# Product of ab with the combined weights: blocks of 480, 192 and 480 tokens in place of four of 288

## Chip, cores and metric

One core of one Trainium2 chip. The time is device microseconds (us) of one execution, median over runs; before the change it is 621.64 us (three runs, 618.79 to 622.22). Lower is better.

## What is computed

Attention over 2 batches, 8 heads and 576 tokens (local for half of the heads, strided for the others) gives x with 1152 rows, the tokens of both batches one after the other, and 512 columns. Two mixtures follow:

```python
a = x @ w1                      # 1152 x 1024
b = x @ w2
x = ((a * b) @ w3) @ w_out      # 1152 x 512
p = probs / (probs.sum(-1, keepdims=True) + 1e-9)
out = 0
for e in range(4):
    out += p[:, e:e+1] * (relu(x @ e1[e]) @ e2[e])
```

## The kernel before

Everything runs on one core in an order written out by hand (a manual schedule): each engine executes its instructions in the order in which the program issues them. Every float32 product is made of three matmuls (`mm3`, lines 303 to 305) on a high and a low part (`hi`, `lo`, type float32r): hi by hi, hi by lo, lo by hi, each with a weight load of its own of 128 x 128. ScalarE (ACT) rounds a number to its high part (a CAST), VectorE (DVE) subtracts it from the number, which leaves the low part.

The stages, with their place in the span:

- Attention, until about 85 us, mixed with the first half of the next stage.
- ab = a * b, feature-major, in units of one block of 128 features (`ft`, 8 of them; two make a *pair*) and half a batch of tokens (288): `ab_block`. A unit is 24 matmuls of 288 columns in two accumulators (`ab_acc`). ACT copies the first one out (L566), DVE multiplies the second one by it (L568), ACT and DVE split the product (L572, L574) into the tile of its batch and pair, `ab_parts`. For pairs 0 to 2 of batch 0 the product is kept whole at first and split later, while batch 1 is computed (`ab_split`, L531 and L532, 1152 columns at once, after units 18, 21 and 24 of 32). Between these operations the program issues, by `advance`, steps of the decoding of the weights that come next: for each 1024-column chunk two ACT operations (L142, L147), DVE's clamp, shift, sign and add (L183, L186, L189, L193), and the split (L201, L230). The raw chunk comes by DMA into one of two buffers, and its load is issued when the add of an earlier chunk is done.
- wc = the product of w3 and w_out (`wc_tile`, 8 tiles of 24 matmuls of 512 columns), 142 to 186 us.
- x3 = wc by ab (`x3_block`), 186 to 237 us: 4 blocks of 288 tokens by 4 blocks of output features, each 8 `ft` by 3 matmuls of 288 columns into one accumulator (`x3_acc`, shown as x_acc in the profile), copied out by ACT (L596). In the last two blocks of tokens the operands of the next stage's first half (tokens 0 to 639) are prepared between them (`early`, 11 steps of splits and subtractions, L616, L617, L621).
- The experts (`Step.first` and `Step.second`), 237 to 613 us, in two halves of 640 and 512 tokens: matmuls of 320 or 256 columns and of 512 columns, with the decoding of the expert weights beside them.

Accumulators of ab, wc and x3 come from one pool of 5 PSUM banks, in turn (`bank`): the sixth accumulator waits until the first of the six has been read. The tiles `ab_parts` lie in two pools of 4 (`big[0]` on the right for batch 0, `big[1]` on the left for batch 1); `big[0]` is released for the operands of the experts (`ops`) when its part of x3 is done.

Of the kernel before, what the change touches and what calls it, by code (L numbers as in the profile page):

```python
# [8 lines left out]
F32 = mybir.dt.float32  # L9
F32R = mybir.dt.float32r  # L10
# [4 lines left out]
ALU = mybir.AluOpType  # L15

B, H, S, D = 2, 8, 576, 64
NT, DM, DFF, E = 1152, 512, 1024, 4
P = 128
# [5 lines left out]
T3 = 3 * NB  # L25
CUT = 288
HB = S // 2
BLK = 384
NBLK = NT // BLK
NTT = NT // P  # L30
# [12 lines left out]
def kernel(  # L43
# [13 lines left out]
    nc = tc.nc  # L57
# [10 lines left out]
    big = [tc.tile_pool(name=f"big{b}", bufs=4, side=side).__enter__() for b, side in enumerate(("right", "left"))]  # L68
# [3 lines left out]
    def bank(name):  # L72
        return ps.tile([P, 512], F32, tag="ps", name=name)

    def unit(name, dtype=F32R):
        return wp.tile([P, 1024], dtype, tag="w", name=name)
# [51 lines left out]
    class Chunk:  # L128
# [68 lines left out]
        def split_hi(self):  # L197
            nonlocal live
            live += 2
            self.hi, self.lo = unit("w_hi"), unit("w_lo")  # L200
            nc.scalar.copy(self.hi, self.f32)  # L201
# [27 lines left out]
        def split_lo(self):  # L229
            nc.vector.tensor_tensor(out=self.lo, in0=self.f32, in1=self.hi.bitcast(F32), op=ALU.subtract)  # L230
            self.done = True
# [61 lines left out]
    def advance(n=1):  # L293

        return all([next(worker, False) for _ in range(n)])
# [5 lines left out]
    def mm3(acc, lhs, rhs, first, last):  # L301
        (lh, ll), (rh, rl) = lhs, rhs
        mm(acc, lh, rh, start=first, stop=False)  # L303
        mm(acc, lh, rl, start=False, stop=False)  # L304
        mm(acc, ll, rh, start=False, stop=last)  # L305
# [212 lines left out]
                nc.vector.tensor_tensor(out=lo, in0=o, in1=hi.bitcast(F32), op=ALU.subtract)  # L518


    ab_hi, ab_lo, whole = {}, {}, {}

    def ab_place(b, pair):
        both = big[b].tile([P, 2, 2, S], F32R, tag="big", name="ab_parts")
        ab_hi[b, pair], ab_lo[b, pair] = both[:, 0], both[:, 1]

    def ab_split(pair):

        ab_place(0, pair)
        hi, lo, ab = ab_hi[0, pair], ab_lo[0, pair], whole.pop(pair)  # L530
        nc.scalar.copy(hi, ab)  # L531
        nc.vector.tensor_tensor(out=lo, in0=ab, in1=hi.bitcast(F32), op=ALU.subtract)  # L532

    def x_split_hi(n):
        x = slice(n * HB, n * HB + HB)
        nc.scalar.copy(x_hi[:, :, x], x_whole[:, :, x])

    def x_split_lo(n):
        x = slice(n * HB, n * HB + HB)
        nc.vector.tensor_tensor(out=x_lo[:, :, x], in0=x_whole[:, :, x], in1=x_hi[:, :, x].bitcast(F32),  # L540
                                op=ALU.subtract)

    def ab_block(b, ft, n):
        t = slice(b * S + n * HB, b * S + n * HB + HB)
        pair, late = ft // 2, b == 0 and ft < 6
        ab = tmp.tile([P, HB], F32, tag="pT", name="ab")
        if n == 0 and ft % 2 == 0:
            if late:
                if pair < 2:
                    parts = big[pair].tile([P, 2, 2, S], F32, tag="big", name="ab_f32")  # L550
                    whole[pair] = parts[:, 0]
                    if pair:
                        whole[2] = parts[:, 1]
            else:
                ab_place(b, pair)
        if late:
            full = whole[pair][:, ft % 2, n * HB:n * HB + HB]
        else:
            full = ab
            hi, lo = (x[b, pair][:, ft % 2, n * HB:n * HB + HB] for x in (ab_hi, ab_lo))  # L560
        for w in range(2):
            acc = bank("ab_acc")[:, :HB]
            for k in range(4):
                mm3(acc, c_w12[ft].parts((w * 4 + k) * P, P), (x_hi[:, k, t], x_lo[:, k, t]), k == 0, k == 3)
            if w == 0:
                nc.scalar.copy(ab, acc)  # L566
            else:
                nc.vector.tensor_tensor(out=full, in0=acc, in1=ab, op=ALU.mult)  # L568
            yield
        if late:  # L570
            return
        nc.scalar.copy(hi, ab)  # L572
        yield
        nc.vector.tensor_tensor(out=lo, in0=ab, in1=hi.bitcast(F32), op=ALU.subtract)  # L574
        yield


# [9 lines left out]
        nc.scalar.copy(raw[:, it], acc)  # L587


    def x3_block(x3, wc, b, n, ot):  # L590
        t = slice(b * S + n * HB, b * S + n * HB + HB)
        acc = bank("x3_acc")[:, :HB]
        for k in range(8):
            ab = tuple(x[b, k // 2][:, k % 2, n * HB:n * HB + HB] for x in (ab_hi, ab_lo))
            mm3(acc, wc[k // 2].parts(512 * (k % 2) + ot * P, P), ab, k == 0, k == 7)
        nc.scalar.copy(x3[:, ot, t], acc)  # L596


# [217 lines left out]
    with tc.manual_schedule():  # L816
# [24 lines left out]
        def run_unit():  # L841

            nonlocal done, rest
            b, ft, i = units[done]
            if done >= 2:
                need(c_w12[ft])
            block = ab_block(b, ft, i)
            for _ in range(2):
                next(rest, None)
                next(block)  # L850
                if done >= 2:
                    advance(1)
                if waiting:
                    waiting.pop().slots_exps()
            rest = block
            done += 1
            if b == i == 1:
                c_w12[ft].free()
# [129 lines left out]
        for n in range(2):  # L988
            acc = bank("ab_acc")[:, :HB]
# [23 lines left out]
        while done < 32:  # L1013
            run_unit()
            if done in (18, 21, 24):
                ab_split({18: 0, 21: 1, 24: 2}[done])
# [7 lines left out]
        wc = [Chunk(None) for _ in range(4)]  # L1024
        for c in c_wout:
            need(c)
        for it in range(8):
# [8 lines left out]
            i = {1: 0, 3: 1, 6: 2}.get(it)  # L1036
# [7 lines left out]
        x3 = xp.tile([P, 4, NT], F32, tag="x_lo", name="x3")  # L1044
# [8 lines left out]
                return kept[:, k]  # L1053
            return ops.tile([P, 2, 320], F32R, tag="op", name=f"b_{name}{i}")[:, :, :n]

        for b, i in ((0, 0), (0, 1), (1, 0), (1, 1)):
            if (b, i) == (1, 0):
                big[0].release()
                ops = ctx.enter_context(tc.tile_pool(name="ops", bufs=14, side="right"))
                early = halves[0].prepare(x3)  # L1060
            for ot in range(4):
                x3_block(x3, wc, b, i, ot)
                advance(1)
                if (b, i) == (1, 0) and ot < 2:
                    next(early)
                elif (b, i) == (1, 1):
                    for _ in range(4):
                        next(early, None)
        for c in wc[:3]:
# [18 lines left out]
        for s, step in enumerate(steps):  # L1088
            need(step.w, 1)
            before = steps[s - 1] if s else None  # L1090
            todo = iter(range(len(before.half.tts)) if s else ())
# [86 lines left out]
```

## Time and profile before

| | us |
|---|---|
| time, median of 3 runs | 621.64 (618.79 to 622.22) |
| the profiled execution, its own time | 618.11 |
| its span, first to last instruction | 616.3 |
| TensorE (PE) busy in the span | 610.0 |
| weight loads (PEld) busy, beside PE | 555.9 |
| VectorE (DVE) busy | 442.4 |
| ScalarE (ACT) busy | 279.3 |

The difference of 1.8 us between the execution's time and its span lies around the span. Matmuls are pipelined, so that the duration of one (0.29 us at 288 columns) is longer than the distance from its start to the next one's (0.13 us): a stage's time is read from starts. Weight loads overlap with matmuls in the same way.

### The profile page before, as it was taken

The page shows a single profiled execution, that of the slowest core. Times are in us where ns is not written, and L with a number is a line of the kernel's source. Part 1 is how long each engine was busy: PE and PEld are TensorE (multiplying, and loading weights), DVE is VectorE, ACT ScalarE, POOL GpSimd, SP SyncE. Part 2 cuts the span into 40 slices and gives each one's busy share as a digit, 9 for nine tenths or more (in the row PEclk, how much of TensorE's full clock was granted, in tenths as well). Part 3 has the DMA queues.
Part 4 walks back from the last instruction along what each step waited for, and adds up shares of the span by engine and source line. Part 5 has one row for each costly group of instructions (what it writes and reads, how often), then busy time and mean ns, then how long its engine had stood idle before and what let it go on. Part 6 is the DMA issues. An engine that isn't in the chain of part 4 may idle for free.

```text
span 616.3 us, 11292 instructions
## 1 busy us (share of the span) xinstructions
PE 610.0 (99%) x4584; PEld 555.9 (90%) x4584; DVE 442.4 (72%) x796; ACT 279.3 (45%) x555; POOL 9.1 (1%) x33
## 2 busy tenths in 40 slices
PE   9999999999999999999999999999999999999997
PEld 5789999998889999998899998999889898989997
DVE  4899987898774237777877987887766665755843
ACT  4779966665644224333443433434343333333320
POOL 4100000000000000000000000000000000000000
PEclk9999999999999999999999999999999999999999
DMA  8986340334524102333545344445585657465411
GB/s 262 350 290 188 139 138 2 112 129 150 198 98 137 58 12 69 137 136 138 194 155 192 124 157 171 160 148 200 188 311 211 213 194 244 166 231 180 151 54 69
DMA packets 28403, 99.44 MB, mean 161 GB/s; under 512 B 2632, under 2 KB 6288, under 8 KB 25920
## 3 DMA queue, kind: packets, MB, share of 16 engines
q1 hardware_dynamic: 28080, 98.43, 45.4%
q8 instruction: 36, 0.59, 0.4%
q10 hardware_dynamic: 272, 0.29, 0.1%
q14 instruction: 15, 0.12, 0.1%
HBM read 79.58 MB, written 19.14 MB: 160 GB/s over the span
## 4 chain that ended last, share of the span: by engine, by line
PE 89%; DVE 4%; ACT 2%; DMA 2%; issue 1%; SPq 0%; POOL 0%; POOLq 0%; ACTq 0%
PE g_acc L303 11%; PE g_acc L304 11%; PE g_acc L305 11%; PE m_a L305 4%; PE m_a L304 4%; PE m_a L303 4%; PE ab_acc L303 4%; PE ab_acc L305 4%; PE ab_acc L304 4%; PE m_b L304 3%; PE m_c L303 3%; PE x_acc L305 3%; PE x_acc L303 3%; PE x_acc L304 3%; PE m_c L304 3%; PE m_b L303 3%
## 5 line engine op out<-in xcount | busy, mean ns | idle before, releaser
L725 ACT ACTIVATE h_hi<-u 128x320 fp32r<-128x320 f32 (+1 forms) x128 | 57.0, 446 | 189.1 <-DVE u L731 189.1
L303 PE MATMUL g_acc<-w_hi,h_hi 128*128 128x512 f32 (+1 forms) x296 | 114.3, 386 | 0.0
L304 PE MATMUL g_acc<-w_lo,h_hi 128*128 128x512 f32 (+1 forms) x296 | 114.2, 386 | 0.0
L305 PE MATMUL g_acc<-w_hi,h_lo 128*128 128x512 f32 (+1 forms) x296 | 113.7, 384 | 0.0
L664 DVE TENSOR_TENSOR w_lo<-raw,w_hi 128x768 fp32r<-128x768 f32 x64 | 69.4, 1085 | 12.5 <-ACT w_hi L662 12.4
L731 DVE TENSOR_TENSOR u<-m_b,u 128x320 f32<-128x320 f32 (+1 forms) x96 | 40.8, 453 | 50.8 <-PE m_b L305 50.8
L303 PE MATMUL ab_acc<-x_hi,w_hi 128*128 128x288 f32 x240 | 71.7, 299 | 0.1
L305 PE MATMUL ab_acc<-x_hi,w_lo 128*128 128x288 f32 x240 | 70.8, 295 | 0.7 <-DVE w_lo L230 0.7
L304 PE MATMUL ab_acc<-x_lo,w_hi 128*128 128x288 f32 x240 | 70.7, 294 | 0.0
L305 PEld LDWEIGHTS g_acc<-w_hi,h_lo 128*128 128x128 f32 x296 | 55.6, 188 | 11.6
L303 PEld LDWEIGHTS g_acc<-w_hi,h_hi 128*128 128x128 f32 x296 | 55.8, 188 | 8.0
L304 PEld LDWEIGHTS g_acc<-w_lo,h_hi 128*128 128x128 f32 x296 | 55.7, 188 | 7.6
L727 DVE SCALAR_TENSOR_TENSOR h_lo<-u,h_hi 128x320 fp32r<-128x320 f32 (+1 forms) x128 | 57.8, 451 | 3.7 <-ACT h_hi L725 1.8
L662 ACT CAST w_hi<-raw 128x768 fp32r<-128x768 f32 x64 | 60.0, 938 | 0.0
L305 PEld LDWEIGHTS ab_acc<-x_hi,w_lo 128*128 128x128 f32 x240 | 45.0, 188 | 1.0 <-DVE w_lo L230 1.0
L303 PEld LDWEIGHTS ab_acc<-x_hi,w_hi 128*128 128x128 f32 x240 | 45.0, 188 | 0.6 <-ACT pT L461 0.4
L304 PEld LDWEIGHTS ab_acc<-x_lo,w_hi 128*128 128x128 f32 x240 | 45.0, 188 | 0.0
L304 PE MATMUL m_b<-b_t,s_hi 128*128 128x320 f32 (+1 forms) x128 | 37.9, 296 | 0.0
L731 DVE TENSOR_TENSOR u<-m_a,u 128x320 f32<-128x320 f32 (+1 forms) x64 | 28.9, 452 | 11.6 <-PE m_a L305 11.6
L664 DVE TENSOR_TENSOR s_lo<-raw,s_hi 128x1024 fp32r<-128x1024 f32 x16 | 19.6, 1226 | 24.4 <-ACT s_hi L662 24.4
L731 DVE TENSOR_TENSOR u<-m_c,u 128x320 f32<-128x320 f32 (+1 forms) x64 | 29.0, 454 | 4.5 <-PE m_c L305 3.9
L741 ACT COPY u<-m_a 128x320 f32<-128x320 f32 (+1 forms) x32 | 12.8, 400 | 41.9 <-PE m_a L305 41.9
(178 smaller groups left out, 1412.8 us busy)
## 6 DMA issues: line engine op xcount, KB each, us to landing
raw<-in_e_dram SPq DMA_DIRECT2D x32, 1024.0 KB, 5.3
raw<-in_w3T_dram SPq DMA_DIRECT2D x8, 1024.0 KB, 5.6
stored<-s_hi SPq DMA_DIRECT2D x16, 512.0 KB, 2.7
stored<-s_lo SPq DMA_DIRECT2D x16, 512.0 KB, 2.7
s_hi<-stored SPq DMA_DIRECT2D x16, 512.0 KB, 5.0
s_lo<-stored SPq DMA_DIRECT2D x16, 512.0 KB, 5.6
raw<-in_w_dram SPq DMA_DIRECT2D x7, 1024.0 KB, 7.2
raw<-in_w_out_dram SPq DMA_DIRECT2D x4, 1024.0 KB, 5.0
```

The lines of the kernel that those rows point to most:

```text
L303: mm(acc, lh, rh, start=first, stop=False)
L304: mm(acc, lh, rl, start=False, stop=False)
L305: mm(acc, ll, rh, start=False, stop=last)
L662: nc.scalar.copy(dst[0], src)
L664: nc.vector.tensor_tensor(out=dst[1], in0=src, in1=dst[0].bitcast(F32), op=ALU.subtract)
L725: nc.scalar.activation(hi, src, AF.Relu)
L727: nc.vector.scalar_tensor_tensor(out=lo, in0=src, scalar=0.0, in1=hi.bitcast(F32), op0=ALU.max, op1=ALU.subtract)
L731: nc.vector.tensor_tensor(out=out, in0=acc, in1=b, op=ALU.add)
L741: nc.scalar.copy(u1, a)
```

## The change

The 1152 tokens of x3 are taken in three blocks: 0 to 479, 480 to 671 and 672 to 1151. The middle block crosses the border of the batches at 576. So that its 192 tokens are side by side in SBUF for one matmul, pairs 0 to 2 keep the last 96 tokens of batch 0 and the first 96 of batch 1 in a tile of their own (`middle`), which is the rest of a batch's `ab_parts` tile once its other 480 tokens are placed: the tile of batch 0 holds the middle of the pair's second `ft`, that of batch 1 that of its first. Pair 3 is stored as before, and takes two matmuls of 96 columns in the middle block. A split of a unit whose tokens lie on both sides of the new border is done in two pieces (96 and 192 columns), the late splits in three (96, 96 and 960).

```diff
+MID = 192
+MAIN = S - MID // 2
...
     def ab_place(b, pair):
-        both = big[b].tile([P, 2, 2, S], F32R, tag="big", name="ab_parts")
-        ab_hi[b, pair], ab_lo[b, pair] = both[:, 0], both[:, 1]
+        both = big[b].tile([P, 4 * S], F32R, tag="big", name="ab_parts")
+        n = MAIN if pair < 3 else S
+        parts_of[b, pair] = both[:, :4 * n].rearrange("p (x k n) -> p x k n", x=2, k=2)
+        if pair < 3:
+            middle[pair, 1 - b] = both[:, 4 * n:].rearrange("p (x n) -> p x n", x=2)
+
+    def ab_pieces(b, ft, t0, n):
...
+    def split_hi(pieces, src):
+        for at, x in pieces:
+            nc.scalar.copy(x[:, 0], src[:, at])
+
+    def split_lo(pieces, src):
+        for at, x in pieces:
+            nc.vector.tensor_tensor(out=x[:, 1], in0=src[:, at], in1=x[:, 0].bitcast(F32), op=ALU.subtract)
...
     def ab_split(pair):
         ab_place(0, pair)
-        hi, lo, ab = ab_hi[0, pair], ab_lo[0, pair], whole.pop(pair)
-        nc.scalar.copy(hi, ab)
-        nc.vector.tensor_tensor(out=lo, in0=ab, in1=hi.bitcast(F32), op=ALU.subtract)
+        if (1, pair) not in parts_of:
+            ab_place(1, pair)
+        ab, main = whole.pop(pair), parts_of[0, pair]
+        for k in range(2):
+            nc.scalar.copy(middle[pair, k][:, 0, :MID // 2], ab[:, k, MAIN:])
+        nc.scalar.copy(main[:, 0], ab[:, :, :MAIN])
+        for k in range(2):
+            x = middle[pair, k][:, :, :MID // 2]
+            nc.vector.tensor_tensor(out=x[:, 1], in0=ab[:, k, MAIN:], in1=x[:, 0].bitcast(F32), op=ALU.subtract)
+        nc.vector.tensor_tensor(out=main[:, 1], in0=ab[:, :, :MAIN], in1=main[:, 0].bitcast(F32), op=ALU.subtract)
...
-    def x3_block(x3, wc, b, n, ot):
-        t = slice(b * S + n * HB, b * S + n * HB + HB)
-        acc = bank("x3_acc")[:, :HB]
-        for k in range(8):
-            ab = tuple(x[b, k // 2][:, k % 2, n * HB:n * HB + HB] for x in (ab_hi, ab_lo))
-            mm3(acc, wc[k // 2].parts(512 * (k % 2) + ot * P, P), ab, k == 0, k == 7)
+    def x3_block(x3, wc, i, ot):
+        t0, n = ((0, MAIN), (MAIN, MID), (MAIN + MID, MAIN))[i]
+        t = slice(t0, t0 + n)
+        acc = bank("x3_acc")[:, :n]
+        todo = []
+        for ft in range(8):
+            w = wc[ft // 2].parts(512 * (ft % 2) + ot * P, P)
+            pair, k = ft // 2, ft % 2
+            if pair == 3:
+                for b in range(B):
+                    a, z = max(t0, b * S), min(t0 + n, b * S + S)
+                    if a < z:
+                        todo.append((w, slice(a - t0, z - t0), parts_of[b, pair][:, :, k, a - b * S:z - b * S]))
+            else:
+                todo.append((w, slice(0, n), middle[pair, k] if i == 1 else parts_of[i // 2, pair][:, :, k]))
+        for i, (w, at, x) in enumerate(todo):
+            mm3(acc[:, at], w, (x[:, 0], x[:, 1]), i == 0, i == len(todo) - 1)
         nc.scalar.copy(x3[:, ot, t], acc)
...
-        for b, i in ((0, 0), (0, 1), (1, 0), (1, 1)):
-            if (b, i) == (1, 0):
+        for i in range(3):
+            if i == 2:
                 big[0].release()
...
             for ot in range(4):
-                x3_block(x3, wc, b, i, ot)
-                advance(1)
-                if (b, i) == (1, 0) and ot < 2:
-                    next(early)
-                elif (b, i) == (1, 1):
+                x3_block(x3, wc, i, ot)
+                advance(1 if i == 1 else 1 + ot % 2)
+                if i == 2:
                     for _ in range(4):
                         next(early, None)
```

On PE, in the x3 stage, before the change, the end of one accumulator's 24 matmuls and the start of the next one's (names with their numbers; `wc_hi` is the last quarter of the combined weights):

```order
L303 MATMUL x3_acc_2499<-ab_parts_1411,wc_hi_2451 128x288
L304 MATMUL x3_acc_2499<-ab_parts_1411,wc_hi_2451 128x288
L305 MATMUL x3_acc_2499<-ab_parts_1411,wc_lo_2452 128x288
L303 MATMUL x3_acc_2526<-ab_parts_1668,w_hi_2279 128x288
L304 MATMUL x3_acc_2526<-ab_parts_1668,w_hi_2279 128x288
L305 MATMUL x3_acc_2526<-ab_parts_1668,w_lo_2280 128x288
```

On PE after the change, where the first block of 480 ends and the middle block begins, then where its pairs 0 to 2 end and pair 3 begins:

```order
L305 MATMUL x3_acc_2613<-ab_parts_1411,wc_hi_2475 128x480
L306 MATMUL x3_acc_2613<-ab_parts_1411,wc_hi_2475 128x480
L307 MATMUL x3_acc_2613<-ab_parts_1411,wc_lo_2476 128x480
L305 MATMUL x3_acc_2642<-ab_parts_1607,w_hi_2303 128x192
L306 MATMUL x3_acc_2642<-ab_parts_1607,w_hi_2303 128x192
...
L307 MATMUL x3_acc_2642<-ab_parts_1916,w_lo_2480 128x192
L305 MATMUL x3_acc_2642<-ab_parts_1411,wc_hi_2475 128x96
L306 MATMUL x3_acc_2642<-ab_parts_1411,wc_hi_2475 128x96
L307 MATMUL x3_acc_2642<-ab_parts_1411,wc_lo_2476 128x96
L305 MATMUL x3_acc_2642<-ab_parts_2080,wc_hi_2475 128x96
L306 MATMUL x3_acc_2642<-ab_parts_2080,wc_hi_2475 128x96
L307 MATMUL x3_acc_2642<-ab_parts_2080,wc_lo_2476 128x96
```

Each row is one weight load and one matmul. The stage had 16 accumulators of 24 matmuls, 384 of 288 columns. It has 8 accumulators of 24 matmuls of 480 columns and 4 of 18 matmuls of 192 and 12 of 96, together 312: 192 of 480, 72 of 192 and 48 of 96. The columns streamed are the same, 110,592.

On ACT in batch 1's part of the ab stage, around the late split of pair 2, before:

```order
L531 CAST ab_parts_1900<-ab_f32_833 128x1152
L572 CAST ab_parts_1748<-ab_1863 128x288
L566 COPY ab_1904<-ab_acc_1906 128x288
L201 CAST w_hi_1920<-t_1820 128x1024
L572 CAST ab_parts_1905<-ab_1904 128x288
```

and after (L551 stands for L572, L564 and L565 for L531, L603 for L566, L203 for L201):

```order
L564 CAST ab_parts_1917<-ab_f32_833 128x96
L564 CAST ab_parts_1916<-ab_f32_833 128x96
L565 CAST ab_parts_1916<-ab_f32_833 128x960
L551 CAST ab_parts_1756<-ab_1878 128x288
L603 COPY ab_1925<-ab_acc_1926 128x288
L203 CAST w_hi_1940<-t_1834 128x1024
L551 CAST ab_parts_1917<-ab_1925 128x96
L551 CAST ab_parts_1917<-ab_1925 128x192
```

The same happens at the late splits of pairs 0 and 1 and at the first half of every `ft` of pairs 0 to 2 of batch 1: 3 by 2 and 6 by 1, 12 operations more on ACT, and the 12 subtractions that belong to them on DVE. SP's and POOL's instructions stay in their order.

## Rows read from the trace of the kernel before

**Rows 1.** The page: busy shares, then the chain that ended last by engine.

```profile
span 616.3 us, 11292 instructions
PE 610.0 (99%) x4584; PEld 555.9 (90%) x4584; DVE 442.4 (72%) x796; ACT 279.3 (45%) x555; POOL 9.1 (1%) x33
...
PE 89%; DVE 4%; ACT 2%; DMA 2%; issue 1%; SPq 0%; POOL 0%; POOLq 0%; ACTq 0%
```

**Rows 2.** The x3 stage as one window: us, busy of each engine, granted clock, DMA.

```profile
185.74:236.63 50.89, 50.89 (x386) 50.88 (x384) 18.41 (x25) 16.03 (x29) 0.00 (x0) 1.00 0.17 63
```

**Rows 3.** Timeline of PE: start, us; matmuls of 512, 288, 320 and 256 columns.

```profile
179.62 0.39 PE L303 MATMUL wc_acc<-w_hi 128*128 128x512 f32 x1
...
185.75 0.29 PE L303 MATMUL x_acc<-ab_parts,w_hi 128*128 128x288 f32 x1
...
236.63 0.31 PE L303 MATMUL m_a<-b_b,w_hi 128*128 128x320 f32 x1
...
240.88 0.31 PE L305 MATMUL m_b<-b_t,s_lo 128*128 128x320 f32 x1
...
575.90 0.28 PE L303 MATMUL m_a<-kept,w_hi 128*128 128x256 f32 x1
...
578.74 0.40 PE L303 MATMUL g_acc<-w_hi,h_hi 128*128 128x512 f32 x1
```

**Rows 4.** Timeline of the weight loads, at two places where matmuls had paused.

```profile
33.68 0.19 PEld L303 LDWEIGHTS ab_acc<-x_hi,w_hi 128*128 128x128 f32 x1
33.79 0.19 PEld L304 LDWEIGHTS ab_acc<-x_lo,w_hi 128*128 128x128 f32 x1
...
142.05 0.19 PEld L303 LDWEIGHTS wc_acc<-w_hi 128*128 128x128 f32 x1
142.16 0.19 PEld L304 LDWEIGHTS wc_acc<-w_lo,w_hi 128*128 128x128 f32 x1
```

**Rows 5.** Timeline of PE: 16 plain float32 products of 288 columns, two records each.

```profile
22.61 8.03 PE L581 MATMUL ab_acc<-x_whole,w_whole 128*128 128x288 f32 x32
```

**Rows 6.** A window of the ab stage, columns as in rows 2.

```profile
105.00:115.00 10.00, 10.00 (x77) 10.00 (x77) 9.94 (x15) 7.65 (x12) 0.00 (x0) 1.00 0.01 2
```

**Rows 7.** Timeline of DVE and of ACT, a split and what follows it.

```profile
111.83 0.45 DVE L574 TENSOR_TENSOR ab_parts<-ab,ab_parts 128x288 fp32r<-128x288 f32 x1
112.20 0.45 DVE L568 TENSOR_TENSOR ab<-ab_acc,ab 128x288 f32<-128x288 f32 x1
...
112.68 0.43 ACT L572 CAST ab_parts<-ab 128x288 fp32r<-128x288 f32 x1 [1.26 <-DVE ab L568]
113.02 0.39 ACT L566 COPY ab<-ab_acc 128x288 f32<-128x288 f32 x1
```

**Rows 8.** All splits of 1152 columns, by line.

```profile
L531 ACT CAST ab_parts<-ab_f x3: 1152/1159/1162, 96.5 to 120.8; 128x1152 fp32r<-128x1152 f32 x3
L532 DVE TENSOR_TENSOR ab_parts<-ab_f,ab_parts x3: 1351/1359/1359, 98.4 to 121.9; 128x1152 fp32r<-128x1152 f32 x3
```

**Rows 9.** Timeline of ACT, DVE and PE at the end of the ab stage.

```profile
134.36 1.19 ACT L142 ACTIVATE raw<-raw 128x1024 int32<-128x1024 uint32 x1 [2.75 <-DMA raw<-in_w3T_dram]
...
136.80 0.38 ACT L566 COPY ab<-ab_acc 128x288 f32<-128x288 f32 x1
...
141.54 0.45 DVE L568 TENSOR_TENSOR ab<-ab_acc,ab 128x288 f32<-128x288 f32 x1
...
137.26 0.37 PE L303 MATMUL ab_acc<-x_hi,w_hi 128*128 128x288 f32 x1
137.47 0.29 PE L304 MATMUL ab_acc<-x_lo,w_hi 128*128 128x288 f32 x1
...
142.11 0.44 PE L303 MATMUL wc_acc<-w_hi 128*128 128x512 f32 x1
```

**Rows 10.** Timeline of ACT and DVE at the end of the x3 stage.

```profile
234.55 0.73 ACT L616 CAST b_t<-x 128x640 fp32r<-128x640 f32 x1 [0.52 <-DVE x L621]
...
235.31 0.82 DVE L617 TENSOR_TENSOR b_t<-x,b_t 128x640 fp32r<-128x640 f32 x1 [0.79 <-ACT b_t L616]
```

More of the change, by code (lines that the diff above doesn't have):

```diff
@@ L518, in put_lo @@
                 nc.vector.tensor_tensor(out=lo, in0=o, in1=hi.bitcast(F32), op=ALU.subtract)
-    ab_hi, ab_lo, whole = {}, {}, {}
+    parts_of, middle, whole = {}, {}, {}
     def ab_place(b, pair):
-        both = big[b].tile([P, 2, 2, S], F32R, tag="big", name="ab_parts")
-        ab_hi[b, pair], ab_lo[b, pair] = both[:, 0], both[:, 1]
+        both = big[b].tile([P, 4 * S], F32R, tag="big", name="ab_parts")
[3 more added lines that the diff above has]
+            middle[pair, 1 - b] = both[:, 4 * n:].rearrange("p (x n) -> p x n", x=2)
@@ new lines, in ab_pieces @@
+    def ab_pieces(b, ft, t0, n):
+        pair, k = ft // 2, ft % 2
+        if pair == 3:
+            return [(slice(0, n), parts_of[b, pair][:, :, k, t0:t0 + n])]
+        pieces = []
+        cut = MAIN if b == 0 else MID // 2
+        for a, z in ((t0, min(cut, t0 + n)), (max(cut, t0), t0 + n)):
+            if a < z:
+                at = slice(a - t0, z - t0)
+                if (a < cut) == (b == 0):
+                    off = 0 if b == 0 else cut
+                    pieces.append((at, parts_of[b, pair][:, :, k, a - off:z - off]))
+                else:
+                    off = b * S - MAIN
+                    pieces.append((at, middle[pair, k][:, :, a + off:z + off]))
+        return pieces
@@ L553, in ab_block @@
                         whole[2] = parts[:, 1]
-            else:
+            elif (b, pair) not in parts_of:
                 ab_place(b, pair)
@@ L559, in ab_block @@
             full = ab
-            hi, lo = (x[b, pair][:, ft % 2, n * HB:n * HB + HB] for x in (ab_hi, ab_lo))
+            pieces = ab_pieces(b, ft, n * HB, HB)
         for w in range(2):
@@ L571, in ab_block @@
             return
-        nc.scalar.copy(hi, ab)
+        split_hi(pieces, ab)
         yield
-        nc.vector.tensor_tensor(out=lo, in0=ab, in1=hi.bitcast(F32), op=ALU.subtract)
+        split_lo(pieces, ab)
         yield
@@ L587, in wc_tile @@
         nc.scalar.copy(raw[:, it], acc)
-    def x3_block(x3, wc, b, n, ot):
-        t = slice(b * S + n * HB, b * S + n * HB + HB)
-        acc = bank("x3_acc")[:, :HB]
-        for k in range(8):
-            ab = tuple(x[b, k // 2][:, k % 2, n * HB:n * HB + HB] for x in (ab_hi, ab_lo))
-            mm3(acc, wc[k // 2].parts(512 * (k % 2) + ot * P, P), ab, k == 0, k == 7)
+    def x3_block(x3, wc, i, ot):
[5 more added lines that the diff above has]
+            w = wc[ft // 2].parts(512 * (ft % 2) + ot * P, P)
+            pair, k = ft // 2, ft % 2
+            if pair == 3:
+                for b in range(B):
+                    a, z = max(t0, b * S), min(t0 + n, b * S + S)
+                    if a < z:
+                        todo.append((w, slice(a - t0, z - t0), parts_of[b, pair][:, :, k, a - b * S:z - b * S]))
+            else:
+                todo.append((w, slice(0, n), middle[pair, k] if i == 1 else parts_of[i // 2, pair][:, :, k]))
+        for i, (w, at, x) in enumerate(todo):
+            mm3(acc[:, at], w, (x[:, 0], x[:, 1]), i == 0, i == len(todo) - 1)
         nc.scalar.copy(x3[:, ot, t], acc)
```

## The prediction

> **What bounds the kernel now.** I read the page first: PE is busy for 610.0 of 616.3 us, and the chain that ended last runs through PE for 89% [rows 1]. An engine that is busy 99% of the span leaves a change two ways to count: it alters what PE itself spends, or it makes PE wait. So I took the stage that the change rewrites as a window. From 185.74 to 236.63 us PE is busy for 50.89 of 50.89 us at full granted clock (1.00, the 2.4 GHz level), DVE for 18.41 and ACT for 16.03 [rows 2]. In x3 nothing but PE ends last. The weight loads are busy 50.88 us there too, so that view can't say whether streaming columns or loading weights sets PE's pace. Starts of matmuls say more.
>
> **The pace of PE by columns.** From 179.62 to 185.75 us there are 27 matmuls of 512 columns: 6.13 / 27 = 227 ns from start to start. The 384 of 288 columns from 185.75 to 236.63 take 132.5 ns each. 29 of 320 columns from 236.63 to 240.88 take 146.6, and 24 of 256 from 575.90 to 578.74 take 118.3 [rows 3]. The first and third give (227 - 146.6) / 192 = 0.419 ns for a column; 288 columns should then take 133.2 and 256 should take 119.8, within 1.5 ns of what they do. So from 256 columns up the line is some 12.5 ns plus 0.419 per column, and 480 columns come to 146.6 + 160 x 0.419 = 213.6 ns.
>
> No row has a float32r matmul under 256 columns, and the change puts 120 there. What the line does below 256 decides. The nearest rows are the weight loads where matmuls had paused and the loads could follow each other freely: from 33.68 to 33.79 us for the first, from 142.05 to 142.16 for the last, 0.11 us apart [rows 4]. There are 13 such pairs, all between 0.108 and 0.110 us apart, and no two loads of 128 x 128 for products of hi and lo parts lie closer. At 288 columns that load is hidden behind 132.5 ns; at 192 the line would want 91.4 ns and at 96 51.2, less than the load.
>
> **The change part by part, x3 stage.**
> - 384 matmuls of 288 columns go: -50.9 us.
> - 192 of 480 come: 192 x 213.6 = 41.0 us.
> - 72 of 192 and 48 of 96 come. If a load takes 110 ns, all 120 take that: 13.2 us. Low bound, the line goes on: 72 x 91.4 + 48 x 51.2 = 9.0 us. High bound for load-bound matmuls, the 118.3 ns of the shortest that is seen: 14.2 us. I take 110 ns, because the loads of the rows are of the very size and type that the new matmuls need.
> - Sum: 41.0 + 13.2 - 50.9 = +3.3 us (bounds -0.9 and +4.3). The saving that is real is 192 x 213.6 against the 320 matmuls that carried the same columns, 320 x 132.5 = 42.4: 1.4 us. The middle block then costs 13.2 where 64 matmuls of 288 cost 8.5: 4.7 us.
>
> The rule that speaks for the change stands in the Trainium skill, TensorE: Matmul & The Clock Gate, section "Back-to-back issue gap": a warm matmul alone has a gap of N / 2.4 + 2.5 ns, and a stream of load and matmul pairs sustains about 81 ns at 128 columns. By the gap alone x3 would be 46.9 us after and 47.0 before, no change; the trace has 132.5 ns at 288 columns where that rule gives 122.5, and no two of these loads under 108 ns, so here the measurement goes before the rule.
>
> **The ab stage.** 12 operations more on ACT and 12 on DVE, with the same elements. A split's 288 columns hold ACT for 0.34 us until the next operation starts (112.68 to 113.02), and DVE for 0.37 (111.83 to 112.20) [rows 7]. Per column ACT takes (1159 - 430) / 864 = 0.84 ns and DVE (1359 - 450) / 864 = 1.05 [rows 7, 8], so 288 columns are 0.24 and 0.30 us of work, and a further operation costs 0.10 us on ACT and 0.07 on DVE when pipelined, 0.19 and 0.15 when it isn't. Twelve: 1.2 and 0.8 us pipelined, 2.3 and 1.8 apart.
>
> Does PE notice? In 105 to 115 us DVE is busy for 9.94 of 10 us [rows 6]. Behind that, ACT waits 2.75 us for a raw chunk by DMA [rows 9], whose load was issued only after DVE's add; what is late on DVE there makes the next load late, and with it the ACT work queued behind it. And PE touches the bound: with five banks its accumulator that starts at 137.26 reuses the one that ACT's copy frees at 136.80 + 0.38 = 137.18, and its first two starts are 0.21 apart rather than 0.13; the first wc accumulator, at 142.11, follows DVE's product that ends at 141.54 + 0.45 = 141.99 [rows 9]. So lateness that reaches 137 us goes to PE nearly in full. Of the 12 pairs four lie after 118 us, and the earlier ones partly fall into DVE's idle time before 105 us and into ACT's. I take +0.7 us; bounds 0 (all absorbed) and 2.0 (nothing is).
>
> **The rest.** The two pools' tiles keep their sizes. ACT's copies of x3 become 8 of 480 and 4 of 192 columns, at most one per 3.3 us; five banks cover them. `early` now runs whole in the last block: its last three steps (a split, a subtraction, a split) follow the third copy, 0.73 + 0.82 ACT and DVE each [rows 10], under 4 us, where PE has 24 x 213.6 ns = 5.1 us of the fourth accumulator to go. Without that cover it would cost at most those 4 us at the first expert step. `advance` has 16 calls in the stage, as before, so weights and their loads keep their order. After 237 us nothing differs.
>
> **Sum.** +3.3 + 0.7 = +4.0 us. On the profiled execution's own 618.11 us (616.3 and 1.8 around it) that is 622.1. It is the fastest of those shown; the median of the runs is 621.64, so I forecast 625.6 us.
>
> **The rivals.**
> - *Short matmuls stay on the line* (loads keep up below 256 columns). For: between 256 and 512 columns the line holds within 1.5 ns, with no sign of a floor. Against: the loads 108 to 110 ns apart [rows 4]. x3 is 0.9 us shorter, with the ab stage's 0.7 the time is 621.4: not slower. It decides where the 120 short matmuls take under 103 ns on average (12.3 us): x3 is then longer by less than 2.4 us, and the sum by less than 3.1.
> - *Short matmuls fall to the plain float32 rate.* The 16 plain products of 288 columns make 32 records in (8.03 - 0.41) us, 31 intervals of 246 ns [rows 5], two per product: 1.7 ns for a column. Then 192 columns cost 328 ns, 96 cost 164 to 220 (two loads): 23.6 + 7.9 to 10.6 us, x3 +21.6 to +24.3, the time about 645 us. For: every float32r matmul here has 256 columns or more, so the trace can't exclude a slower rate below. Against: nothing in it shows such a step. The Trainium skill, FP8 and Floating Point Precision, section "TensorE Precision Notes", has true float32 in 4 passes and the reduced kind cut to about 22 bits, and ties neither to the number of columns.
> - *The ab stage's chain loses a whole round*: the late add delays one chunk's load so that ACT's queue, 3 us of wait already, slips in two rounds. Price some 3 us on top, 628 us. For: PE is at the bound twice. Against: in 105 to 115 us ACT is busy for 7.65 of 10 us [rows 6], which leaves room for operations of 0.1 us.
>
> **How the numbers follow.** The forecast 0.65, the line 0.14, the plain rate 0.15, the lost round 0.06. About 0.5%, 3.1 us, is what a measurement of this kernel can tell from no change. The three runs of before lie 3.4 us apart, so of the forecast's +4.0 (3.3 to 6.3 by its bounds) some 0.42 of its 0.65 show as slower and 0.23 as the same. With the two dear rivals slower is 0.63; the same is 0.23 + 0.10 of the line = 0.33; faster 0.04. The range goes from 620.8 (the line, and the fast runs) to 629.0 (both upper bounds of the sum, 627.9, and a run's spread); it leaves the plain rate out.
>
> **What would show it.** A window on x3 of about 54 us against 50.9; starts 0.21 us apart at 480 columns, 0.11 at 192 and at 96 alike. The same distance at both is the mark of the load; 0.09 and 0.05 would be the line, 0.3 the plain rate. The wc stage should begin some 0.7 us later than 142.11, with the rest of the program shifted and unchanged. The prediction is wrong if x3 isn't longer than before, or if the experts' stage changes length.

## The result

The changed kernel takes 623.56 us (median of 16 runs, 622.34 to 627.09), the kernel before 618.58 us over its 16 runs (616.97 to 622.22); the ratio is 1.0071, interval 1.005 to 1.0091. It is slower by 0.7%: 4.4 us by the ratio, 5.0 by the two medians. Three runs had given the kernel before 621.64; with more of them its median is 3.1 us lower, so 4.0 us was forecast against a base that sat high, and the forecast of 625.6 lies 2.0 us above the measured time. Runs of one kernel differ by up to 5 us, mostly with their mean granted clock: the changed kernel's runs at 0.999 or 1.00 took 622.3 to 623.1 us but for one of 625.55, those at 0.991 to 0.997 took 624.0 to 627.1.

The page of the changed kernel, busy shares and chain, for [rows 1]:

```profile
span 620.2 us, 11168 instructions
PE 614.7 (99%) x4512; PEld 555.0 (89%) x4512; DVE 443.2 (71%) x808; ACT 279.8 (45%) x563; POOL 9.1 (1%) x33
...
PE 84%; DVE 6%; DMA 4%; ACT 4%; issue 2%; SPq 0%; POOL 0%; DVEq 0%; ACTq 0%; POOLq 0%
```

72 matmuls fewer, and 3.9 us more of span. PE is busy 4.7 us longer: the time is in PE, not in a wait. This execution took 622.71 us, so 2.5 us lie around its span, where 1.8 did before; the experiment with the pieces comes back to this. The x3 stage of the changed kernel in three windows, its first block, the middle and the last (columns as in [rows 2]):

```profile
185.23:206.18 20.95, 20.95 (x98) 18.01 (x96) 8.47 (x13) 6.25 (x9) 0.00 (x0) 1.00 0.27 101
206.18:219.50 13.32, 13.32 (x121) 13.32 (x120) 1.23 (x1) 2.47 (x5) 0.00 (x0) 1.00 0.20 80
219.50:240.55 21.05, 21.05 (x99) 18.09 (x99) 8.63 (x11) 6.48 (x11) 0.00 (x0) 1.00 0.00 1
```

Together 55.32 us against 50.89 [rows 2]: +4.43, more than the whole difference of the spans (3.9). The outer blocks take 42.0 us for 192 matmuls, 218.2 and 219.3 ns each; the middle 13.32 us for 120, 111 ns each. In the middle the load's time (third number, PEld) is as long as the window; by itself that is no sign of the load, since at 288 columns it filled the window too [rows 2]. The distances say more. The timeline of PE in the middle block, where the columns go from 480 to 192, and from 192 to 96 (start, duration in us):

```profile
205.96 0.38 PE L307 MATMUL x_acc<-ab_parts,wc_lo 128*128 128x480 f32 x1
206.18 0.25 PE L305 MATMUL x_acc<-ab_parts,w_hi 128*128 128x192 f32 x1
...
207.83 0.28 PE L305 MATMUL x_acc<-ab_parts,w_hi 128*128 128x192 f32 x1
207.94 0.28 PE L306 MATMUL x_acc<-ab_parts,w_hi 128*128 128x192 f32 x1
208.05 0.28 PE L307 MATMUL x_acc<-ab_parts,w_lo 128*128 128x192 f32 x1
...
208.79 0.28 PE L305 MATMUL x_acc<-ab_parts,wc_hi 128*128 128x96 f32 x1
208.90 0.27 PE L306 MATMUL x_acc<-ab_parts,wc_hi 128*128 128x96 f32 x1
209.01 0.28 PE L307 MATMUL x_acc<-ab_parts,wc_lo 128*128 128x96 f32 x1
```

0.11 us from start to start at 192 columns and at 96 alike: half the columns save nothing. That is the distance at which the loads of [rows 4] followed each other.

Outside x3 little differs. The wc stage begins at 141.65 us, where it was 142.11 [rows 9]: earlier by 0.5 us, not later. The experts take 376.3 us from their first matmul to their last in both traces.

### The profile page after: what moved, and what is told of

Same layout as the page of the kernel before. It is cut to its first block, busy times and chain, and to the rows that moved or that the text cites. A ratio compares the mean times of both kernels' runs of the same rounds, so it can differ in the third digit from the quotient of the medians.

```text
span 620.2 us, 11168 instructions
## 1 busy us (share of the span) xinstructions
PE 614.7 (99%) x4512; PEld 555.0 (89%) x4512; DVE 443.2 (71%) x808; ACT 279.8 (45%) x563; POOL 9.1 (1%) x33
## 4 chain that ended last, share of the span: by engine, by line
PE 84%; DVE 6%; DMA 4%; ACT 4%; issue 2%; SPq 0%; POOL 0%; DVEq 0%; ACTq 0%; POOLq 0%
PE g_acc L305 11%; PE g_acc L306 11%; PE g_acc L307 11%; PE m_a L307 4%; PE m_a L306 4%; PE m_a L305 4%; PE x_acc L307 3%; PE x_acc L306 3%; PE x_acc L305 3%; PE m_b L306 3%; PE m_c L305 3%; PE m_c L306 3%; PE m_b L305 3%; PE m_c L307 3%; PE m_b L307 3%; PE wc_acc L305 2%
## 5 line engine op out<-in xcount | busy, mean ns | idle before, releaser
L779 DVE TENSOR_TENSOR u<-m_b,u 128x320 f32<-128x320 f32 (+1 forms) x96 | 40.8, 452 | 51.2 <-PE m_b L307 51.2
```

Source lines behind the costliest of these rows:

```text
L779: nc.vector.tensor_tensor(out=out, in0=acc, in1=b, op=ALU.add)
```

## The experiments

The theory: a float32r matmul with a load of 128 columns costs the longer of its load, 111 ns, and some 12.5 ns plus 0.419 ns a column; so 120 matmuls under 256 columns lose more than 72 fewer matmuls save. The rivals: storing the middle side by side, or reading it so, costs the time; a matmul under 256 columns has a floor that isn't the load; the extra pieces of the splits cost it in the ab stage.

**The pieces of the splits alone.** The kernel before, with its splits cut as in the change:

```diff
-        nc.scalar.copy(hi, ab)
+        pieces = (slice(0, 96), slice(96, HB)) if b and n == 0 and pair < 3 else (slice(0, HB),)
+        for at in pieces:
+            nc.scalar.copy(hi[:, at], ab[:, at])
...
+        parts = [(slice(k, k + 1), slice(cut, S)) for k in range(2)] + [(slice(0, 2), slice(0, cut))]
```

> The kernel before with only the splits cut into pieces (12 operations more on ACT, 12 on DVE), storage and x3 as before. Theory of the prediction: these make PE late at the end of the ab stage, so the time from the first ab matmul of hi and lo parts to the first wc matmul (108.4 us before, 107.4 after the change) grows by 0.7 us, and the time by 0.1%. Rival (the ab stage's part is nothing, the changed kernel's start of wc was even 0.5 us earlier): that stretch stays within the 0.5 us by which it moves anyway, and the time is the same.

Ratio 1.0017, interval 0.999 to 1.0044: no difference that shows in the time. The stretch from the first ab product to wc, as one window:

```profile
37.67:145.09 107.42, 106.93 (x1088) 104.56 (x1081) 95.64 (x169) 79.97 (x211) 0.00 (x0) 1.00 0.41 140
```

107.4 us with the pieces, as in the changed kernel (34.23 to 141.65, 107.4). Without them it is 108.4 before, and 107.3 and 106.8 in the two experiments below that keep the old storage. The trace of the kernel before is the longest by a wait at its start: at 41.42 us, some 50 us ahead of the first cut split, PE waited 0.9 us for a low part from DVE, in this trace alone. From the first matmul of batch 1 (91.17 us before, 90.36 after) to wc, the part in which splits are cut, it is 50.9 us before, 51.3 after the change and 51.5 with the pieces alone, but also 51.3 and 50.9 in the two experiments without them. These differ by one wait, at the accumulator at 137 us that the prediction named. PE of the kernel before, ACT and PE of the changed kernel, PE of the experiment with the old splits and blocks of 480, 192 and 480:

```profile
40.39 0.30 PE L304 MATMUL ab_acc<-x_lo,w_hi 128*128 128x288 f32 x1
41.42 0.40 PE L305 MATMUL ab_acc<-x_hi,w_lo 128*128 128x288 f32 x1 [0.73 <-DVE w_lo L230]
...
136.32 0.39 ACT L603 COPY ab<-ab_acc 128x288 f32<-128x288 f32 x1
136.33 0.29 PE L307 MATMUL ab_acc<-x_hi,w_lo 128*128 128x288 f32 x1
136.76 0.40 PE L305 MATMUL ab_acc<-x_hi,w_hi 128*128 128x288 f32 x1
...
141.22 0.29 PE L305 MATMUL ab_acc<-x_hi,w_lo 128*128 128x288 f32 x1
141.71 0.40 PE L303 MATMUL ab_acc<-x_hi,w_hi 128*128 128x288 f32 x1 [0.20 <-ACT ab L566]
```

In the changed kernel the copy ends at 136.71 us and PE starts 0.43 us after its last start, 0.3 late. Without the pieces it is late there by 0.4 in one trace and by under 0.1 in two, with them by 0 to 0.5 in seven. So a share of the pieces in it doesn't stand out.

The pieces do cost time at another place. An execution's time less its span is 1.74 to 1.84 us in 23 runs of the kernel before, 2.14 to 2.60 in the 10 runs with the pieces alone and 2.08 to 2.65 in the changed kernel's 16. It is 1.8 in the two experiments with the old splits and 2.1 to 2.6 in all others. So some 0.7 us come with the pieces, outside the span. The traces show nothing there; why it comes is open.

**A middle block of 512 tokens.** One number of the change, so 320, 512 and 320:

```diff
-MID = 192
+MID = 512
```

> The change with a middle block of 512 tokens: blocks of 320, 512 and 320, pair 3 of the middle in two of 256. The number of matmuls is that of the change (312) and so are the columns, but none has under 256. Theory (a float32r matmul costs the greater of a weight load of 111 ns and 12.5 ns plus 0.419 ns per column): x3 takes 192 x 146.6 + 72 x 227 + 48 x 118.3 ns = 50.2 us, against 55.3 in the changed kernel and 50.9 before; the time is 0.8 us under before's. Rival (the extra time comes with storing the middle side by side, or with crossing from tile to tile): x3 stays near 55 us.

x3 as a window, and PE where its middle goes from 512 to pair 3's 256 columns:

```profile
184.98:235.52 50.54, 50.54 (x313) 47.36 (x312) 17.49 (x24) 15.26 (x25) 0.00 (x0) 1.00 0.17 63
```

```profile
202.79 0.39 PE L306 MATMUL x_acc<-ab_parts,w_hi 128*128 128x512 f32 x1
203.02 0.39 PE L307 MATMUL x_acc<-ab_parts,w_lo 128*128 128x512 f32 x1
203.25 0.28 PE L305 MATMUL x_acc<-ab_parts,wc_hi 128*128 128x256 f32 x1
203.37 0.29 PE L306 MATMUL x_acc<-ab_parts,wc_hi 128*128 128x256 f32 x1
```

The same 312 matmuls, the same columns, the same crossing of batches, stored side by side: 50.54 us against 55.32. So neither the storage nor the crossing costs time in x3; the short matmuls do. The time is 1.0014 of before's (0.9986 to 1.0041), no difference; x3 itself is 0.35 us shorter than before, less than the 0.7 expected, because 512 columns took 232 ns here.

**The blocks without the side-by-side storage.** The kernel before with blocks of 480, 192 and 480; every pair takes two matmuls of 96 in the middle:

```diff
+        t0, n = ((0, 480), (480, 192), (672, 480))[i]
...
+            for b in range(B):
+                a, z = max(t0, b * S), min(t0 + n, b * S + S)
+                if a < z:
+                    ab = tuple(x[b, k // 2][:, k % 2, a - b * S:z - b * S] for x in (ab_hi, ab_lo))
+                    todo.append((w, slice(a - t0, z - t0), ab))
```

> The kernel before with blocks of 480, 192 and 480 tokens and nothing stored side by side: in the middle block every pair takes two matmuls of 96 columns, 192 short matmuls in place of 120. Theory of the load: 192 x 218.5 + 192 x 111 ns = 63.3 us for x3, and the time 12.4 us over before. Rival (a matmul's fixed cost and its columns alone): 192 x 218.5 + 192 x 52 = 51.9 us. The start of wc should be that of the kernel before, since splits and storage are.

Neither came: one run took 652.94 us, and x3 81.28. The windows, first all of x3, show why (the granted clock is the third number from the end):

```profile
190.17:271.45 81.28, 81.28 (x386) 74.90 (x384) 18.32 (x25) 15.21 (x25) 0.00 (x0) 0.77 0.10 39
...
206.00:211.00 5.00, 5.00 (x25) 4.30 (x24) 2.66 (x5) 1.29 (x2) 0.00 (x0) 1.00 0.39 157
211.00:215.00 4.00, 4.00 (x36) 3.97 (x35) 0.00 (x0) 0.56 (x1) 0.00 (x0) 0.94 0.00 0
215.00:219.00 4.00, 4.00 (x21) 4.00 (x21) 0.00 (x0) 0.32 (x1) 0.00 (x0) 0.50 0.02 4
...
252.00:254.00 2.00, 2.00 (x10) 1.67 (x9) 0.00 (x0) 0.00 (x0) 0.00 (x0) 0.97 0.00 0
```

From about 211 us PE had only matmuls of 96 columns; soon after, the granted clock fell to 0.50 (the 1.2 GHz level), and it came back to full at 252.1 us, after the matmuls of 480 columns had begun again at 248.7. PE counts as busy for all of it: this view's busy share doesn't show the fall, the clock column does. At half clock the same matmuls stand 213 ns apart, at full clock 112, as the first of them did. PE's timeline at full clock and after the fall:

```profile
211.35 0.28 PE L303 MATMUL x_acc<-ab_parts,w_hi 128*128 128x96 f32 x1
211.46 0.28 PE L304 MATMUL x_acc<-ab_parts,w_hi 128*128 128x96 f32 x1
...
230.18 0.41 PE L303 MATMUL x_acc<-ab_parts,w_hi 128*128 128x96 f32 x1
230.39 0.41 PE L304 MATMUL x_acc<-ab_parts,w_hi 128*128 128x96 f32 x1
```

Nor did wc start where it does before, but at 146.59 us: the granted clock was 0.50 in attention too, from 20.0 to 26.8 us, and the first ab product of hi and lo parts came at 39.32 us in place of 33.68. That is about the rest of this run's time: x3 is 30.4 us longer, and the run lies 34.5 above the median of 618.43 that 23 runs of the kernel before had beside it.

**The short matmuls between long ones.** The same work and the same 192 matmuls of 96 columns, issued between those of the first block:

```diff
+        for _, at, w, ab, first, last in sorted(todo, key=lambda x: x[0]):
+            mm3(at, w, ab, first, last)
...
+        for i in ((0, 1), (2,)):
```

> The kernel with blocks of 480, 192 and 480 and nothing stored side by side again (192 short matmuls of 96 columns), but the matmuls of the middle block issued between those of the first: three of 480 columns, then six of 96. Theory: the granted clock fell to half in the run before because matmuls of 96 columns alone, each with its load, followed one another for 21 us; between matmuls of 480 columns it stays at full, and x3 takes 192 x 218.5 + 192 x 112 ns = 63.5 us, 12.6 over before. Rival (short matmuls themselves draw the clock down, or cost 213 ns each): about 81 us again.

x3 as a window, and some of the timeline:

```profile
188.12:251.69 63.57, 63.57 (x386) 57.41 (x385) 18.32 (x25) 15.30 (x25) 0.00 (x0) 1.00 0.13 50
```

```profile
200.27 0.38 PE L304 MATMUL x_acc<-ab_parts,w_hi 128*128 128x480 f32 x1
200.49 0.38 PE L305 MATMUL x_acc<-ab_parts,w_lo 128*128 128x480 f32 x1
...
200.86 0.27 PE L305 MATMUL x_acc<-ab_parts,w_lo 128*128 128x96 f32 x1
200.97 0.28 PE L303 MATMUL x_acc<-ab_parts,w_hi 128*128 128x96 f32 x1
201.09 0.28 PE L304 MATMUL x_acc<-ab_parts,w_hi 128*128 128x96 f32 x1
```

Full clock throughout, 63.57 us against 63.5 expected. At full clock the blocks with 192 short matmuls cost 12.7 us more than before's x3; the other 17.7 us of the last run's x3 came with the lower clock.

**Half the load.** The changed kernel with weights of 64 columns in the middle block; the other 64 output features of those tokens are left out and set to zero:

```diff
+        m = 64 if i == 1 else P
...
-            w = wc[ft // 2].parts(512 * (ft % 2) + ot * P, P)
+            w = wc[ft // 2].parts(512 * (ft % 2) + ot * P, m)
```

> The changed kernel with weights of 64 columns in the middle block: only the first 64 of each 128 output features are computed there, and the others are set to zero. Theory of the load: loading half the columns takes about half of 111 ns, so matmuls of 192 columns fall from 112 ns to the line's 92 and those of 96 from 112 to some 55; x3 is 42.0 + 6.6 + 2.6 = 51.2 us against 55.3. Rival (a floor per matmul that doesn't depend on what is loaded): 112 ns at both, x3 unchanged.

x3, and PE where its middle goes from 192 to 96 columns:

```profile
189.22:240.36 51.14, 51.14 (x313) 45.20 (x312) 18.32 (x25) 15.19 (x25) 0.00 (x0) 1.00 0.17 62
```

```profile
211.49 0.25 PE L305 MATMUL x_acc<-ab_parts,w_hi 128*64 128x192 f32 x1
211.58 0.25 PE L306 MATMUL x_acc<-ab_parts,w_hi 128*64 128x192 f32 x1
211.67 0.25 PE L307 MATMUL x_acc<-ab_parts,w_lo 128*64 128x192 f32 x1
...
211.86 0.22 PE L307 MATMUL x_acc<-ab_parts,wc_lo 128*64 128x96 f32 x1
211.92 0.22 PE L305 MATMUL x_acc<-ab_parts,wc_hi 128*64 128x96 f32 x1
211.97 0.22 PE L306 MATMUL x_acc<-ab_parts,wc_hi 128*64 128x96 f32 x1
```

51.14 us, where 51.2 was expected. With half the weights the same 192 columns take 0.09 us and 96 columns 0.057 (means 89 and 57 ns). With half the load the floor of 111 ns is gone, and the columns count again. At 96 columns the line alone gives 52.7 ns, so 57 doesn't show whether the new floor is half the old one or lower. The edit also halves the output rows of these matmuls; a floor that goes with the rows, and not with the load, isn't excluded by it. For the load speaks that loads alone stood 108 to 110 ns apart where matmuls had paused [rows 4].

**Two other sizes.** A middle of 384 tokens (three blocks of 384, pair 3 in 192) and one of 256 (448, 256, 448, pair 3 in 128), again by the one number.

> The change with a middle block of 384 tokens: three blocks of 384, pair 3 of the middle in two of 192. Theory of the load, with the line: 264 x 173.4 + 48 x 112 ns = 51.2 us for x3. If the surplus that 480 columns showed in the changed kernel (218.5 ns where the line has 213.6) grows with the columns, 384 columns take some 176 ns and x3 51.8 us. Rival of the first prediction's kind (only columns and a fixed cost count): 264 x 173.4 + 48 x 91.4 = 50.2 us.

> The change with a middle block of 256 tokens: 448, 256 and 448, pair 3 of the middle in two of 128. Theory of the load, with the line: 192 x 200.2 + 72 x 118.3 + 48 x 112 ns = 52.3 us for x3; with a surplus of 4 to 5 ns at 448 columns 53.2 us. The 128-column matmuls stand 112 ns apart, as those of 96 and 192 did. Rival without a load's floor: 128 columns take 66 ns, x3 50.1 to 51 us.

x3 as a window, with 384 and with 256:

```profile
186.47:237.95 51.48, 51.48 (x313) 51.47 (x312) 17.96 (x25) 15.29 (x25) 0.00 (x0) 1.00 0.16 62
...
189.04:242.33 53.29, 53.29 (x314) 49.95 (x313) 18.32 (x25) 15.22 (x25) 0.00 (x0) 1.00 0.16 60
```

With 384 that is 0.3 from either expectation (51.2 and 51.8 us), with 256 within 0.1 of the 53.2 with the surplus. Short matmuls stood 110 ns apart at 192 columns and 111 at 128 (medians). The long ones took 175 ns on average at 384 columns, 1.6 over the line's 173.4, and 206 at 448, 5 above its 200.2.

**Where the operand lies.** The kernel with a middle of 512, one high part moved to a tile of the first pool:

```diff
+    apart = const.tile([P, MID], F32R, name="apart")
...
+            if (pair, b) == (0, 1):
+                middle[pair, 1 - b] = Two(apart, both[:, 4 * n + MID:])
```

> The kernel with the middle block of 512 tokens, where matmuls of 512 columns in x3 stood 232 ns apart, and 227 in the stages around it. Here the high part of pair 0's first ft in the middle lies in a tile of the first pool (2 KB beside the masks), its low part where it was. If the surplus of 5 ns comes from where the moving operand lies in SBUF, the two matmuls that stream that high part (hi by hi, lo by hi) fall to 227 ns in each of the four accumulators, and the hi by lo stays at 232. If it comes from the number of columns in this stage, whatever they are read from, all stay at 232.

PE at the three matmuls with that operand:

```profile
202.26 0.40 PE L305 MATMUL x_acc<-apart,w_hi 128*128 128x512 f32 x1
202.50 0.39 PE L306 MATMUL x_acc<-ab_parts,w_hi 128*128 128x512 f32 x1
202.73 0.39 PE L307 MATMUL x_acc<-apart,w_lo 128*128 128x512 f32 x1
202.96 0.39 PE L305 MATMUL x_acc<-ab_parts,w_hi 128*128 128x512 f32 x1
```

Still 0.23 to 0.24 us, x3 50.55 us: that place isn't the cause of the surplus. Nor is the new storage: in the experiment with blocks of 480, 192 and 480 and the old storage, the first block's matmuls of 480 columns took 217.8 ns at full clock.

## Why the prediction was right, point by point

- *The short matmuls, 13.2 us at 110 ns*: 13.32 us, 111 ns, the same at 192 and 96 columns. Shown by the changed kernel's rows; that the load is its cause, by the run with half the load together with [rows 4]. The Trainium skill, TensorE: Matmul & The Clock Gate, section "LDWEIGHTS (loading the stationary operand)", gives a load's ns as its columns over 1.2, an estimate of 107 ns for 128 columns. The traces agree within 6 ns, with 108 to 112 at full clock.
- *192 matmuls of 480 columns, 41.0 us*: 42.0. This term was mis-sized, 213.6 ns where 218.7 were measured. The line through 320 and 512 columns came from other stages; in x3 it holds within 2 ns at 256, 320 and 384 columns and is passed by about 5 at 448, 480 and 512. So the saving that the prediction called real, 1.4 us, was 0.4.
- *The ab stage, +0.7 us*: the place was right, the size not shown. A cut CAST costs ACT 94 ns more and a cut subtraction DVE 70, as priced, and PE was late by 0.3 us at the accumulator that was named, but by as much in a trace without the pieces. The wc stage didn't begin 0.7 us later. The pieces' 0.7 us outside the span was in no term of the sum; that it has the size of this one is chance.
- *The low bound of the short matmuls, 9.0 us*: its 91.4 and 51.2 ns go down from the 118.3 measured at 256 columns; the line as written gives 92.9 and 52.7, and 9.2 us. Nothing hangs on it.
- The total came near by luck. The spans differ by 3.9 us: +4.4 in x3, and -0.5 up to the start of wc, which comes of the 0.9 us that PE waited at 41.42 us in the trace of the kernel before. The forecast had +3.3 and +0.7.
- *Rivals.* The line going on below 256 columns and the plain float32 rate are both out by the 111 ns. The lost round in the ab stage did not come. The `early` steps were hidden as argued, but closely: DVE's last ends at 239.91 us, the experts begin at 240.54.

The gap rule of the Trainium skill, TensorE: Matmul & The Clock Gate, section "Back-to-back issue gap", set aside in the prediction, would have had x3 unchanged. It lost to the rows here too: x3 is 4.4 us longer.

## What to carry to other kernels

Fewer matmuls aren't cheaper if some of them get shorter than their own weight load: read the load's distance where loads follow each other freely, and cut blocks so that every matmul streams longer than that. Here 312 matmuls of at least 256 columns took 50.5 us and 312 with 120 short ones 55.3, for the same columns. The former is 0.35 us less than before's x3 with its 384 matmuls of 288, which the time doesn't show. And a sum made stage by stage should have its line from the same stage where one is to be had.

## What was not expected of the hardware

- While PE had only matmuls of 96 columns, each with a load of 128, the granted clock fell from 1.00 to 0.50 although PE counts as busy throughout; with the same matmuls issued between matmuls of 480 columns it stayed at 1.00. At 0.50 load and matmul stood 213 ns apart, at 1.00 112, so what sets this distance slows with the clock. The changed kernel's middle block, 72 matmuls of 192 and 48 of 96, kept full clock in its profile.
- In x3 matmuls of 448, 480 and 512 columns take 206, 219 and 232 ns on average; 512 take 227 in wc. In the experts they take 229 on average, between 224 and 236, so x3 isn't alone in this. Neither a tile elsewhere nor the old storage changed it; what does is open.
- 12 more operations each on ACT and DVE, from splits cut in pieces, left the span as it was (medians at full clock 616.1 us with, 616.0 without), and some 0.7 us more around it.
